# Attention and two gated layers in one kernel: state scores in column tiles, w_out converted one stage earlier

## The chip, the cores and the metric

The kernel runs on one core of a Trainium2 chip. The metric is the device time of one execution in microseconds (us), the median of several runs of the same program. Inside a core TensorE (PE in the profile) multiplies matrices, VectorE (DVE) and ScalarE (ACT) work element by element, GpSimd (POOL) does a little of the same, and the queue of SyncE (SP) issues the DMA transfers. [...]

## The reference

Eight batches, eight heads, 512 tokens x of 64 numbers and 32 state tokens per head. `xread` lets each x token read the 32 states, `sread` lets each state read the 512 x tokens. Both go through a gated layer (512 to 1536 to 512) and then through a second layer (512 to 2048 to 512):

```python
scores  = scale * x @ state.T        # first softmax, over 32 states
xread   = softmax(scores) @ state
scores2 = scale * state @ x.T        # second softmax, over 512 x tokens
sread   = softmax(scores2) @ x
x  = concat(xread, sread).reshape(4352, 512)
x  = (sigmoid(x @ w_gate) * (x @ w_val)) @ w_out
out = g(x @ w2_in) @ w2_out          # g: quadratic between -1 and 1, else 0 or h
```

The weights come in double precision. The kernel turns them into float32 itself, and most products are made of three fp32r products of high and low parts.

## The kernel before, in words

The eight batches are done in two groups of four (group 0, group 1). The program is a row of stages that share TensorE's queue:

1. **The start.** The attention of group 0. Its order is written out by hand in the table `PRE` (line 1320): each word is a step, a letter and the pair of heads. `st` transposes the state, `X` transposes x (`att_x`), `S` makes scores (`att_s`), `m` takes the maximum over 32 states and subtracts it (`att_m`), `x` is exp, `e` copies the raw scores to SBUF for the second softmax (`att_e`), `n` normalizes, `T` and `L` transpose the probabilities and split them in a high and a low part, `M` and `K` multiply the state into w_gate and w_val (`m_pair`, `m_low`), `Q` is the first quarter of the first gated step, and `p` and `j` convert a weight block.
2. **The gated pass of group 0** (`gated(0)`, line 594): 24 steps of 24 matmuls of 512 columns (line 582). Even steps end in two sigmoids on ACT (line 639), odd ones in two products on DVE (line 642) that go to HBM. In every odd step two M pairs are made (line 549) for a later step. They use the two PSUM tiles that the even step's sigmoids have just read.
3. **The output pass of group 0** (`output1(0)`, line 729): 96 slots of 6 matmuls with w_out (lines 713 to 715), whose moving side is split by ACT (`oh_hi`, line 680) and DVE (`oh_lo`, line 682). Into its slots go the attention of group 1 (`at_items`) and the second softmax of group 0 and then of group 1 (`sr_items`: `sr_e`, `sr_u`, `sr_r`, `sr_p`). `slot1` (line 1504) hands them out.
4. The gated pass and the output pass of group 1, the state tokens, and the whole second layer follow. They end at the span's end.

A weight block is converted by the class `Weights` in four moves: `load` (a DMA of 512 KB into one of `CB[0]` buffers `wraw`), `parts` (two ACT instructions, lines 158 and 159, into a buffer `ca` and one of two buffers `cy`), `join` (two DVE instructions, lines 165 and 169), and for w_out `high` (ACT, line 182) and `low` (DVE, line 188) into tiles that stay in SBUF. There are 24 blocks of w_gate and w_val, 12 of w_out, 16 of w2_out and 16 of w2_in, and they are done in the order of the list `weights.todo`.

`att_s` takes the x tokens as the stationary side, 128 at a time, and a block-diagonal matrix `bd` of states as the moving side: 16 float32 matmuls of 64 columns for a pair of heads, scores with x tokens on the partitions. `sr_e` then transposes them back (line 377), since the second softmax needs the state on the partitions.

Of the kernel before, what the change touches and what calls it, by code (L numbers as in the profile page):

```python
# [25 lines left out]
def attention_moe_moe_kernel(  # L26
# [28 lines left out]
    nc = tc.nc  # L55
# [40 lines left out]
    CB = [3, 4, 2]  # L96
    p1 = pool("p1", stack=st_p1)
    sd = p1.tile([128, 2, HP, 128], F32, tag="sd", name="sd")
    pe2 = pool("pe2", stack=st_e2)
    bd = pe2.tile([128, H, 4, 2, N], F32, tag="bd", name="bd")  # L100
# [7 lines left out]
    att_bufs, stn_tag = (4, 2, 2), "stn"  # L108
# [12 lines left out]
    ]  # L121
    w2_dram = [tc.dram_tile([128, 512], F32, name=f"w2_dram_{i}") for i in range(NM2)]
# [8 lines left out]
    class Weights:  # L131
# [91 lines left out]
    at_t = {}  # L223

    def load_state(bg):
        t = att.tile([128, H, 2, D], F32, tag=stn_tag, name="stn", bufs=att_bufs[0] if bg else 1)
        for b in range(4):
            o = slice(32 * b, 32 * b + 32)
            for r in range(2):
                nc.sync.dma_start(  # L230
                    out=t[o, :, r], in_=state[4 * bg + b].rearrange("h n d -> n h d")
                )
        return t

    def make_state(t, bg, k):


        ps = ps_tile(k).rearrange("p a f -> p (a f)")
        for h in range(H):
            nc.tensor.transpose(ps[:, 128 * h : 128 * h + 128], t[:, h], ident)  # L240

        def make_bd():
            for r in range(2):
                o = slice(64 * r, 64 * r + 64)
                bv = bd[o, :, :, r].rearrange("p h b n -> p (h b) n")
                v = ps[o].rearrange("p (c n) -> p c n", n=N)
                if r == 0:
                    nc.vector.tensor_copy(bv, v)
                else:
                    nc.scalar.activation(out=bv, in_=v, func=AF.Copy)  # L250

        def make_sd():
            for r in range(2):
                o = slice(64 * r, 64 * r + 64)
                v = ps[o].rearrange("p (k r c) -> p k r c", k=HP, r=2)[:, :, r]
                if r == 0:
                    nc.scalar.activation(out=sd[o, bg], in_=v, func=AF.Copy)
                else:
                    nc.vector.tensor_copy(sd[o, bg], v)

        return make_bd, make_sd
# [26 lines left out]
    def att_s(bg, hp, c, k):  # L288
        if c == 0:
            sc_t[bg, hp] = ps_tile(k)  # L290
        ps = sc_t[bg, hp].rearrange("p g (q e b n) -> p g q e b n", q=2, e=2, b=4)
        xT = xT_t.pop((bg, hp, c)).rearrange("p b (e q s) -> p b e q s", e=2, q=2)
        for b2 in range(2):
            for e in range(2):
                for q2 in range(2):
                    nc.tensor.matmul(
                        out=ps[:, q2, :, e ^ b2, 2 * c + b2],
                        lhsT=xT[:, b2, e, q2],
                        rhs=bd[:, 2 * hp + e, 2 * c + b2],
                        start=True,  # L300
                        stop=True,
                    )

# [4 lines left out]
    def att_m(bg, hp):  # L308
        pv = sc_t[bg, hp].rearrange("p g (c n) -> p (g c) n", n=N)
        m = att.tile([128, 32, 1], F32, tag="m", name="m", bufs=2)  # L310
        nc.vector.tensor_reduce(out=m, in_=pv, axis=AX.X, op=ALU.max)
# [4 lines left out]
        t = t_of(bg, hp).rearrange("p (q b) e n -> p q b e n", q=4)  # L316
        pv = pv.rearrange("p (q e b) n -> p q e b n", q=4, e=2)
        mv = m.to_broadcast([128, 32, N]).rearrange("p (q e b) n -> p q e b n", q=4, e=2)
        for e in range(2):
            nc.vector.tensor_tensor(  # L320
                out=t[:, :, :, e], in0=pv[:, :, e], in1=mv[:, :, e], op=ALU.subtract
            )
# [4 lines left out]

    def att_e(bg, hp):
        e2 = pe2.tile([128, 2, 512], F32, tag="e2", name="e2", bufs=4)
        nc.scalar.activation(out=e2, in_=sc_t.pop((bg, hp)), func=AF.Copy)  # L330
        e2_t[bg, hp] = e2
# [39 lines left out]
    def sr_e(bg, hp, k):  # L371
        s = e2_t[bg, hp]
        sv = s.rearrange("p g (q e c) -> p (g q) e c", q=2, e=2)
        ps = ps_tile(k)
        for e in range(2):
# [7 lines left out]
        post.append(lambda: sr_exp(s, ps, m2, r2))  # L383

    def sr_exp(s, ps, m2, r2):
        for e in range(2):
            nc.scalar.activation(
                out=s[:, e],
                in_=ps[:, e],
# [20 lines left out]
    def sr_u(bg, hp, k):  # L410
        e2 = e2_t.pop((bg, hp))
        ps = ps_tile(k)
        for e in range(2):
            for q in range(4):
                c = slice(128 * q, 128 * q + 128)
                nc.tensor.transpose(ps[:, e, c], e2[:, e, c], ident)
# [112 lines left out]
    def m_pair(k):  # L529
# [13 lines left out]
        for i in range(2):  # L543
            for b2 in range(2):
                for e in range(2):
# [5 lines left out]
                        lhsT=sd[o, bg, 2 * hq + i, 32 * b : 32 * b + 32],  # L551
# [38 lines left out]
    def gated(bg, begun=None, hooks={}):  # L590
# [4 lines left out]
        for i in range(4 * NQ):  # L595
# [19 lines left out]
            for _ in range(2):  # L615
                if i % 2 == 0 or i == 1:
                    split_ws()
                if i % 2 == 0:
                    if len(weights.first) < 2:
                        weights.parts()  # L620
                elif len(weights.mid) < weights.ahead:
                    weights.join()
# [1190 lines left out]
```

## Time and profile before

| what | value |
| --- | --- |
| median of 3 runs | 1452.36 us (1449.73 to 1454.36) |
| the profiled execution | 1457.21 us, its span 1455.4 us |
| PE busy | 1400.8 us, 96% |
| DVE busy | 896.3 us, 62% |
| ACT busy | 742.1 us, 51% |
| DMA engines busy | 60.9% |

The shares say that TensorE is the engine to watch, but they are means over stages with different limits. [...] Times below are counted from the span's start.

### The profile page before, as it was taken

What the parts mean: (1) busy time and instruction counts of PE and PEld (TensorE: products, weight loads), DVE (VectorE), ACT (ScalarE), POOL (GpSimd) and SP (SyncE); (2) the same over time, 40 slices, a digit from 0 to 9 for tenths busy, and PEclk for the clock granted to TensorE, in tenths of its full rate; (3) what the DMA queues carried; (4) which work ended last, traced back from release to release, by engine and by line L of the source; (5) the groups of instructions that cost most, each with busy time, mean ns of one, the idle gap of its engine ahead of it and who ended that gap; (6) DMA issues with size and microseconds to landing.
All of it is one profiled execution on the core that took longest, in us unless ns stands there. A gap on an engine that the chain in (4) does not pass through costs nothing. (4 is left out here: it accounts for less than half of the span.)

```text
span 1455.4 us, 23194 instructions
## 1 busy us (share of the span) xinstructions
PE 1400.8 (96%) x9008; PEld 1192.4 (82%) x9008; DVE 896.3 (62%) x1321; ACT 742.1 (51%) x1099; POOL 239.6 (16%) x140
## 2 busy tenths in 40 slices
PE   7899998899989999999999999999999999999997
PEld 7577776788757778789977888878879999999997
DVE  5555566657446653542266665656577887877775
ACT  6644555545346542322156777778864443434432
POOL 2000000000000000000007758698800000000000
PEclk9999998999999999999999999999999999999999
DMA  7355658757748985889265556966459334333342
GB/s 243 133 198 187 231 184 294 253 189 230 255 151 321 329 291 192 322 320 380 77 234 216 213 213 232 343 228 223 193 184 358 120 123 145 126 127 123 118 132 87
DMA packets 152669, 310.06 MB, mean 213 GB/s; under 512 B 16112, under 2 KB 83696, under 8 KB 151152
## 3 DMA queue, kind: packets, MB, share of 16 engines
q1 hardware_dynamic: 152296, 308.33, 60.9%
q8 instruction: 70, 1.15, 0.3%
q14 instruction: 39, 0.32, 0.1%
q10 hardware_dynamic: 264, 0.26, 0.1%
HBM read 181.01 MB, written 127.53 MB: 212 GB/s over the span
## 5 line engine op out<-in xcount | busy, mean ns | idle before, releaser
L1069 PE MATMUL u<-yc,wt 128*128 128x512 f32 x1344 | 310.4, 392 | 5.8 <-ACT m L1077 3.9
L1069 PEld LDWEIGHTS u<-yc,wt 128*128 128x128 f32 x1344 | 253.2, 189 | 62.1 <-ACT m L1077 5.5
L582 PE MATMUL ps<-at_hi,M 128*128 128x512 f32 x768 | 243.8, 393 | 0.9 <-ACT sg L639 0.9
L582 PEld LDWEIGHTS ps<-at_hi,M 128*128 128x128 f32 x768 | 144.1, 188 | 51.1 <-issue 19.3
L804 POOL TENSOR_TENSOR w2c<-w2c 128x256 f32<-128x256 f32 (+2 forms) x38 | 37.0, 987 | 723.6 <-DMA w2c<-w_dram 718.7
L713 PE MATMUL ps<-oh_hi,wo 128*128 128x512 f32 x368 | 150.3, 408 | 4.0 <-ACT oh_hi L680 4.0
L714 PE MATMUL ps<-oh_lo,wo 128*128 128x512 f32 x368 | 146.8, 399 | 5.6 <-DVE oh_lo L682 5.6
L582 PE MATMUL ps<-at_lo,M 128*128 128x512 f32 x384 | 149.9, 390 | 1.1 <-DVE at_lo L363 1.1
L715 PE MATMUL ps<-oh_hi,wo 128*128 128x512 f32 x368 | 145.9, 396 | 0.0
L1137 PE MATMUL o<-w,hc 128*128 128x256 f32 x476 | 136.0, 286 | 1.5 <-ACT w L927 1.5
L1139 PE MATMUL o<-w,hc 128*128 128x256 f32 x476 | 136.1, 286 | 1.2 <-DVE hc L1185 1.2
L1138 PE MATMUL o<-w,hc 128*128 128x256 f32 x476 | 136.2, 286 | 1.1 <-DVE w L804 1.1
L1139 PE MATMUL o<-wt,hc 128*128 128x256 f32 x476 | 134.8, 283 | 0.7 <-DVE hc L1185 0.7
L1138 PE MATMUL o<-wt,hc 128*128 128x256 f32 x476 | 134.7, 283 | 0.0
L1137 PE MATMUL o<-wt,hc 128*128 128x256 f32 x476 | 134.7, 283 | 0.0
L1181 ACT ACTIVATE hc<-hc 128x512 fp32r<-128x512 f32 (+1 forms) x108 | 64.9, 602 | 136.6 <-DMA hc<-hd_dram 124.2
L567 DVE TENSOR_TENSOR M<-ps,M 128x1024 fp32r<-128x1024 f32 x48 | 56.8, 1219 | 107.2 <-ACT M L561 107.2
L991 POOL TENSOR_TENSOR yc<-yr,yc 128x1024 fp32r<-128x1024 f32 x49 | 116.4, 2416 | 11.2 <-ACT yc L988 11.2
L1029 DVE SCALAR_TENSOR_TENSOR sg<-u,sg 128x512 f32<-128x512 f32 x96 | 66.3, 690 | 71.5 <-ACT u L1028 70.7
L1181 ACT ACTIVATE hc<-hs 128x512 fp32r<-128x512 f32 (+1 forms) x144 | 80.1, 597 | 48.7 <-DVE hs L1178 48.1
L1027 ACT ACTIVATE u<-sg,half 128x512 f32<-128x512 f32 x96 | 66.4, 692 | 71.2 <-DVE sg L1047 69.7
L682 DVE TENSOR_TENSOR oh_lo<-oh_lo,oh_hi 128x1024 fp32r<-128x1024 f32 x48 | 58.6, 1223 | 64.8 <-ACT oh_hi L680 64.8
(154 smaller groups left out, 2798.7 us busy)
## 6 DMA issues: line engine op xcount, KB each, us to landing
hd_dram<-sg SPq DMA_DIRECT2D x64, 512.0 KB, 5.0
h_dram<-sg SPq DMA_DIRECT2D x48, 512.0 KB, 4.3
oh_lo<-h_dram SPq DMA_DIRECT2D x48, 512.0 KB, 5.7
hc<-hd_dram SPq DMA_DIRECT2D x96, 256.0 KB, 4.3
yr<-y_dram SPq DMA_DIRECT2D x32, 512.0 KB, 6.8
wraw<-in_moe_w_out_dram SPq DMA_DIRECT2D x28, 512.0 KB, 5.2
ws_dram<-w SPq DMA_DIRECT2D x24, 512.0 KB, 6.0
ws<-ws_dram SPq DMA_DIRECT2D x24, 512.0 KB, 8.9
```

Source lines behind the costliest of these rows:

```text
L582: nc.tensor.matmul(out=ps[bp][:, b2], lhsT=M[:, l, b2, c], rhs=a[:, b2], start=(hq == 0 and j == 0), stop=(hq == 1 and j == 2),)
L713: nc.tensor.matmul(out=ps, lhsT=wh[:, c], rhs=hi, start=first, stop=False)
L714: nc.tensor.matmul(out=ps, lhsT=wh[:, c], rhs=lo, start=False, stop=False)
L715: nc.tensor.matmul(out=ps, lhsT=wl[:, c], rhs=hi, start=False, stop=last)
L991: low_on.tensor_tensor(out=t[:, 1, :n], in0=src, in1=f32(t[:, 0, :n]), op=SUB)
L1027: nc.scalar.activation(out=s, in_=c, func=AF.Relu, bias=half, scale=0.5)
L1029: return lambda: nc.vector.scalar_tensor_tensor(out=o, in0=s, scalar=1.0, in1=c, op0=ALU.min, op1=ALU.max)
L1069: nc.tensor.matmul(out=pm[j], lhsT=a, rhs=b, start=not more and k == 0 and i == 0, stop=k == 1 and i == 2, skip_group_check=more,)
L1137: nc.tensor.matmul(out=ps, lhsT=wh, rhs=vh, start=start and i == 0, stop=False)
L1138: nc.tensor.matmul(out=ps, lhsT=wh, rhs=vl, start=False, stop=False)
L1139: nc.tensor.matmul(out=ps, lhsT=wl, rhs=vh, start=False, stop=last)
L1181: nc.scalar.activation(out=get(j)[0], in_=raw(j), func=AF.Copy)
```

## The change

It has three parts.

**Scores by state token.** `att_s` now takes the state as the stationary side (64 rows by 32 columns, a tile of the array) and x as the moving side (256 columns): 16 matmuls on eight such tiles. Their result has the states on the partitions, so the second softmax can use it as it is: `sr_e` loses its transposes and reads SBUF. The first softmax needs the x tokens on the partitions, so a new step `A` (`att_a`) transposes the copy in SBUF that `E` (`att_e`) makes, and `m` waits for it. The block-diagonal matrix and its copies go; `sT`, the transposed state, takes their place and that of `sd`.

**State doubled on chip.** The state is loaded once (four DMAs, on ACT's queue for group 0) and copied by DVE, not loaded twice.

**w_out one stage earlier.** Blocks 4 to 11 of w_out are converted among the blocks of w_gate and w_val in `gated(0)`, put into HBM as float32 (`wof_dram`), loaded again in the first slots of the output pass (`load_wo`) and split there (`split_wo`). Blocks 0 to 3 come last in the gated pass. The blocks of w2_out follow from there. In `gated(0)` three blocks per two steps are converted, not two. The slots of the output pass that convert are now every fourth from slot 22 on, and its attention items start at slot 8, not 16. `PRE` has a new order.

```diff
-    CB = [3, 4, 2]
+    CB = [3, 5, 2]
...
         def high(self):
-            if self.mid and opened:
+            if self.mid and (opened or getattr(self.mid[0][1], "early", False)):
...
     def make_state(t, bg, k):
+        nc.vector.tensor_copy(t[:, :, 1], t[:, :, 0])
         ps = ps_tile(k).rearrange("p a f -> p (a f)")
         for h in range(H):
             nc.tensor.transpose(ps[:, 128 * h : 128 * h + 128], t[:, h], ident)
...
+        v = ps.rearrange("p (h c) -> p h c", h=H)
+        nc.vector.tensor_copy(sT[bg][:, : H // 2], v[:, : H // 2])
+        return lambda: nc.scalar.activation(
+            out=sT[bg][:, H // 2 :], in_=v[:, H // 2 :], func=AF.Copy
+        )
...
-    def att_s(bg, hp, c, k):
...
+    def att_s(bg, hp, k):
+        sc_t[bg, hp] = ps = ps_tile(k)
+        xT = [xT_t.pop((bg, hp, c)) for c in range(2)]
+        for e in range(2):
+            for b in range(4):
+                for r in range(2):
+                    o = slice(64 * r, 64 * r + 64)
+                    i = 256 * (e ^ (b % 2))
                     nc.tensor.matmul(
-                        out=ps[:, q2, :, e ^ b2, 2 * c + b2],
-                        lhsT=xT[:, b2, e, q2],
-                        rhs=bd[:, 2 * hp + e, 2 * c + b2],
+                        out=ps[32 * b : 32 * b + 32, r, i : i + 256],
+                        lhsT=sT[bg][o, 2 * hp + e, 32 * b : 32 * b + 32],
+                        rhs=xT[b // 2][o, b % 2, 256 * e : 256 * e + 256],
...
+    def att_a(bg, hp, k):
+        e2 = e2_t[bg, hp]
+        ps = ps_tile(k)
+        for e in range(2):
+            for q in range(4):
+                nc.tensor.transpose(ps[:, e, 128 * q : 128 * q + 128], e2_part(e2, e, q), ident)
+        a_t[bg, hp] = ps
...
-    def sr_e(bg, hp, k):
+    def sr_e(bg, hp):
         s = e2_t[bg, hp]
-        sv = s.rearrange("p g (q e c) -> p (g q) e c", q=2, e=2)
-        ps = ps_tile(k)
-        for e in range(2):
-            for q in range(4):
-                nc.tensor.transpose(ps[:, e, 128 * q : 128 * q + 128], sv[:, q, e], ident)
         m2 = srd.tile([128, 2], F32, tag="m2", name="m2", bufs=2)
-        nc.vector.tensor_reduce(out=m2, in_=ps, axis=AX.X, op=ALU.max)
+        nc.vector.tensor_reduce(out=m2, in_=s, axis=AX.X, op=ALU.max)
...
+            if bg == 0:
+                weights.low()
+                weights.high()
+                for _ in range(2 if i % 2 and i < 18 else 1):
+                    weights.join()
+                for _ in range(1 if i % 2 or i > 17 else 2):
+                    weights.parts()
...
+        dst.early = i < 2
+        dst.kind = "raw" if i >= 4 else "wo"
...
+    def load_wo(i):
+        nc.sync.dma_start(out=f32(wo_tiles(i)[1]), in_=wof_dram[i])
+
+    def split_wo(i):
+        hi, lo = wo_t[i]
+        nc.scalar.activation(out=hi, in_=f32(lo), func=AF.Copy)
+        nc.vector.tensor_tensor(out=lo, in0=f32(lo), in1=f32(hi), op=ALU.subtract)
...
-        "st bd X00 X01 S00 sd S01 p0 X10 X11 m0 x0 j0 e0 p1 S10 n0 S11 m1 X20 j1 X21 S20 x1 "
...
+        "st sb X00 X01 X10 S0 E0 X11 A0 p0 m0 S1 E1 X21 A1 p1 X20 X30 j0 S2 x0 m1 x1 E2 j1 n0 p2 "
...
-    weights.todo += [job_m(i) for i in range(4 * NQ)]
+    weights.todo += [job_m(i) for i in range(8)]
+    for i in range(8, 4 * NQ):
+        weights.todo += [job_wo(i // 2)] * (i % 2 == 0) + [job_m(i)]
+    weights.todo += [job_wo(i) for i in range(4)]
...
+        if n < 8:
+            load_wo(4 + n)
+        if n % 2 and 5 <= n < 20:
+            split_wo((n + 3) // 2)
...
-        if n % (2 if n < 28 or n >= 60 else 8) == 0:
+        if n >= 22 and n % 4 == 2:
             weights.slot()
```

TensorE's queue at the start, up to the second pair of heads: `stn` is the state, `xa` the x tokens, `e` the raw scores in SBUF. Before, then now:

```order
1 L240 MATMUL ps_213<-ident,stn 128x128 x8
2 L281 MATMUL ps_224<-ident,xa 128x128 x8
3 L281 MATMUL ps_238<-ident,xa 128x128 x8
4 L296 MATMUL ps_255<-bd,xT 128x2x32 x16
5 L281 MATMUL ps_278<-ident,xa 128x128 x8
6 L281 MATMUL ps_292<-ident,xa 128x128 x8
7 L296 MATMUL ps_327<-bd,xT 128x2x32 x16
```

```order
1 L238 MATMUL ps_229<-ident,stn 128x128 x8
2 L263 MATMUL ps_240<-ident,xa 128x128 x8
3 L263 MATMUL ps_254<-ident,xa 128x128 x8
4 L263 MATMUL ps_268<-ident,xa 128x128 x8
5 L280 MATMUL ps_279<-xT,sT 32x256 x16
6 L263 MATMUL ps_298<-ident,xa 128x128 x8
7 L306 MATMUL ps_309<-ident,e_296 128x128 x8
8 L280 MATMUL ps_326<-xT,sT 32x256 x16
```

The scores (L296, now L280) are followed by transposes of their copy (L306), with an x transpose of the next pair between them.

ACT's queue in two steps of the gated pass (an odd one and the even one behind it), with what each instruction waits for: `ca` and `cy` are the two instructions of `parts`, `sg` the sigmoids, `M` the copies of an M pair. Before, then now:

```order
50 L158 ACTIVATE ca<-wraw 128x512 [waits DMAHW6_49,DMAHW5_49,DMAHW4_49]
51 L159 ACTIVATE cy<-wraw 128x512 [waits DVE_49]
52 L158 ACTIVATE ca<-wraw 128x512 [waits DMAHW7_49,DMAHW1_49,DMAHW0_49]
53 L159 ACTIVATE cy<-wraw 128x512 [waits DVE_49]
54 L639 ACTIVATE sg<-ps_721 128x1024 [waits PE_49]
55 L639 ACTIVATE sg<-ps_722 128x1024 [waits PE_49]
56 L561 ACTIVATE M_786<-ps_777 128x1024 [waits PE_49]
```

```order
49 L158 ACTIVATE ca<-wraw 128x512 [waits DMAHW5_49,DMAHW1_49]
50 L159 ACTIVATE cy<-wraw 128x512 [waits DVE_49]
51 L158 ACTIVATE ca<-wraw 128x512 [waits DMAHW4_49,DMAHW3_49,DMAHW0_49]
52 L159 ACTIVATE cy<-wraw 128x512 [waits DVE_49]
53 L158 ACTIVATE ca<-wraw 128x512 [waits DMAHW6_49,DMAHW5_49,DMAHW2_49]
54 L159 ACTIVATE cy<-wraw 128x512 [waits DVE_49]
55 L642 ACTIVATE sg<-ps_774 128x1024 [waits PE_49]
56 L642 ACTIVATE sg<-ps_775 128x1024 [waits PE_49]
57 L556 ACTIVATE M_844<-ps_835 128x1024 [waits PE_49]
```

A third conversion stands ahead of the two sigmoids, and each conversion waits for a transfer and for DVE.

ACT's queue where the gated pass ends and the output pass begins: `wo` are the halves of w_out, `oh_hi` the split of the moving side, `e` the exp of the second softmax. Before, then now:

```order
130 L680 ACTIVATE oh_hi<-oh_lo_1371 128x1024
131 L182 ACTIVATE wo_0_1819<-ca 128x512
132 L182 ACTIVATE wo_1_1840<-ca 128x512
133 L182 ACTIVATE wo_2_1861<-ca 128x512
134 L158 ACTIVATE ca<-wraw 128x512
135 L159 ACTIVATE cy<-wraw 128x512
136 L680 ACTIVATE oh_hi<-oh_lo_1578 128x1024
137 L387 ACT_TABLE_LOAD
138 L387 ACTIVATE e_321,r_1839<-ps_1827,m_1836 128x512 x2
139 L182 ACTIVATE wo_3_1874<-ca 128x512
140 L158 ACTIVATE ca<-wraw 128x512
141 L159 ACTIVATE cy<-wraw 128x512
```

```order
152 L695 ACTIVATE oh_hi<-oh_lo_1483 128x1024
153 L182 ACTIVATE wo_2_1963<-ca 128x512
154 L182 ACTIVATE wo_3_1967<-ca 128x512
155 L695 ACTIVATE oh_hi<-oh_lo_1704 128x1024
156 L695 ACTIVATE oh_hi<-oh_lo_1891 128x1024
157 L678 ACTIVATE wo_4_1974<-wo_4_1975 128x512
158 L383 ACT_TABLE_LOAD
159 L383 ACTIVATE e_296,r_2040<-e_296,m_2037 128x512 x2
160 L678 ACTIVATE wo_5_1987<-wo_5_1988 128x512
```

The `ca` and `cy` instructions (L158, L159) are gone from between the splits; a single split per block of w_out (L678) is left.

## Rows read from the trace of the kernel before

**Rows 1.** Windows by stage: length, PE, PEld, DVE, ACT, POOL busy, PEclk, DMA.
```profile
0.00:57.50 57.50, 42.86 (x333) 34.61 (x333) 35.70 (x47) 37.63 (x47) 10.56 (x19) 1.00 0.60 192
57.50:201.30 143.80, 143.45 (x860) 105.36 (x861) 76.83 (x84) 67.13 (x86) 0.00 (x0) 1.00 0.57 198
201.30:401.20 199.90, 185.57 (x1417) 150.94 (x1415) 122.70 (x196) 101.54 (x148) 0.00 (x0) 0.96 0.72 238
```

**Rows 2.** Waits of PE, 201.3 to 401.2: us in total, times, longest.
```profile
PE ps L281 <- ACT ev L720: 4.2, 1, 4.2
PE ps L713 <- ACT oh_hi L680: 4.0, 2, 2.2
PE ps L714 <- DVE oh_lo L682: 3.0, 3, 1.1
```

**Rows 3.** Windows behind three waits of the output pass, columns as in Rows 1.
```profile
218.00:222.50 4.50, 3.14 (x7) 2.34 (x8) 3.71 (x6) 0.77 (x2) 0.00 (x0) 0.65 0.99 345
228.90:236.00 7.10, 6.30 (x15) 4.73 (x16) 6.73 (x9) 6.11 (x10) 0.00 (x0) 0.55 0.67 230
258.90:264.00 5.10, 5.07 (x19) 4.40 (x20) 2.58 (x8) 4.38 (x8) 0.00 (x0) 0.53 0.87 297
```

**Rows 4.** Timeline of ACT, output pass: start, length, instruction, idle before and releaser.
```profile
223.96 0.66 ACT L158 ACTIVATE ca<-wraw 128x512 f32<-128x512 f32 x1 [5.20 <-DMA wraw<-in_moe_w_out_dram]
...
256.75 0.66 ACT L158 ACTIVATE ca<-wraw 128x512 f32<-128x512 f32 x1 [1.53 <-DMA wraw<-in_moe_w_out_dram]
```

**Rows 5.** Timeline of PE, output pass: transposes of the second softmax, and scores.
```profile
252.28 1.03 PE L377 MATMUL ps<-ident,e 128*128 128x128 f32 x8
253.07 0.48 PE L713 MATMUL ps<-oh_hi,wo 128*128 128x512 f32 x1
...
282.61 3.68 PE L296 MATMUL ps<-bd,xT 128*128 128x64 f32 x32
```

**Rows 6.** Timeline of PE, gated pass: two M pairs between steps' matmuls.
```profile
96.18 0.39 PE L582 MATMUL ps<-at_hi,M 128*128 128x512 f32 x1
96.50 1.95 PE L549 MATMUL ps<-ca,sd 64*32 64x512 f32 x32
98.38 0.50 PE L582 MATMUL ps<-at_hi,M 128*128 128x512 f32 x1
```

**Rows 7.** Timeline of the start: SP's queue, PE, DVE.
```profile
0.75 3.86 SPq L230 DMA_DIRECT2D stn<-in_state_dram  x8
...
6.45 1.94 PE L240 MATMUL ps<-ident,stn 128*128 128x128 f32 x8 [6.45 <-DMA stn<-in_state_dram]
...
15.70 1.22 DVE L311 TENSOR_REDUCE m<-ps 128x32 f32<-128x1024 f32 x1 [1.46 <-PE ps L296]
...
49.49 1.23 DVE L363 TENSOR_TENSOR at_lo<-ps,at_hi 128x1024 fp32r<-128x1024 f32 x1 [0.79 <-ACT at_hi L358]
...
57.50 2.01 PE L549 MATMUL ps<-ca,sd 64*32 64x512 f32 x32 [2.57 <-ACT sg L639]
```

**Rows 8.** Timeline of the gated pass: SP's queue, ACT, DVE and PE.
```profile
102.21 0.42 SPq L148 DMA_DIRECT2D wraw<-in_moe_w_val_dram  x1
...
103.54 0.42 SPq L148 DMA_DIRECT2D wraw<-in_moe_w_val_dram  x1
...
101.80 0.69 DVE L169 SCALAR_TENSOR_TENSOR ca<-ca,cy 128x512 uint32<-128x512 uint32 x1
...
105.42 0.68 ACT L158 ACTIVATE ca<-wraw 128x512 f32<-128x512 f32 x1 [2.21 <-DMA wraw<-in_moe_w_val_dram]
...
103.74 2.35 DVE L642 TENSOR_TENSOR sg<-sg,ps 128x1024 f32<-128x1024 f32 x2
...
109.48 1.95 PE L549 MATMUL ps<-ca,sd 64*32 64x512 f32 x32
...
115.19 0.42 SPq L148 DMA_DIRECT2D wraw<-in_moe_w_val_dram  x1
...
120.70 0.66 ACT L158 ACTIVATE ca<-wraw 128x512 f32<-128x512 f32 x1 [4.50 <-DMA wraw<-in_moe_w_val_dram]
```

More of the change, by code (lines that the diff above doesn't have):

```diff
@@ L121, in attention_moe_moe_kernel @@
     ]
+    wof_dram = {i: tc.dram_tile([128, 512], F32, name=f"wof_dram_{i}") for i in range(4, NM1)}
     w2_dram = [tc.dram_tile([128, 512], F32, name=f"w2_dram_{i}") for i in range(NM2)]
@@ L228, in load_state @@
             o = slice(32 * b, 32 * b + 32)
[L229 to L232, printed above, removed]
+            eng.dma_start(out=t[o, :, 0], in_=state[4 * bg + b].rearrange("h n d -> n h d"))
         return t
     def make_state(t, bg, k):
+        nc.vector.tensor_copy(t[:, :, 1], t[:, :, 0])
         ps = ps_tile(k).rearrange("p a f -> p (a f)")
@@ L302, in att_s, with att_e, e2_part @@
                     )
+    def att_e(bg, hp):
+        e2 = pe2.tile([128, 2, 512], F32, tag="e2", name="e2", bufs=4)
+        nc.scalar.activation(
+            out=e2.rearrange("p e (r f) -> p r e f", r=2),
+            in_=sc_t.pop((bg, hp)).rearrange("p r (e f) -> p r e f", e=2),
+            func=AF.Copy,
+        )
+        e2_t[bg, hp] = e2
+    def e2_part(e2, e, q):
+        o = 256 * (q % 2) + 128 * (q // 2)
+        return e2[:, e, o : o + 128]
+    def att_a(bg, hp, k):
[5 more added lines that the diff above has]
+        a_t[bg, hp] = ps
     def t_of(bg, hp):
@@ L315, in att_m @@
             )
[L316 to L322, printed above, removed]
+        nc.vector.tensor_tensor(
+            out=t_of(bg, hp).rearrange("p c e n -> p e c n"),
+            in0=ps.rearrange("p e (c n) -> p e c n", n=N),
+            in1=m.to_broadcast([128, 32, N]).rearrange("p (e c) n -> p e c n", e=2),
+            op=ALU.subtract,
+        )
     def att_exp(bg, hp):
@@ L614, in gated @@
                             m_item(1 - v)
[L615 to L621, printed above, removed]
-                    weights.join()
+            if bg == 0:
+                weights.low()
+                weights.high()
+                for _ in range(2 if i % 2 and i < 18 else 1):
+                    weights.join()
+                for _ in range(1 if i % 2 or i > 17 else 2):
+                    weights.parts()
+            else:
+                for _ in range(2):
+                    if i % 2 == 0 or i == 1:
+                        split_ws()
+                    if i % 2 == 0:
+                        if len(weights.first) < 2:
+                            weights.parts()
+                    else:
+                        weights.join()
             weights.load()
@@ L1336, in attention_moe_moe_kernel @@
             nc.gpsimd.memset(par[32 * b : 32 * b + 32, e : e + 1], float(b % 2 == e))
+    for c in range(4, 6):
+        load_xa(0, c // 2, c % 2)
+        weights.load(c - 2)
     q_ps = []
@@ L1358, in attention_moe_moe_kernel @@
             att_exp(0, n)
-        elif c == "e":
+        elif c == "E":
             att_e(0, n)
@@ L1438, in attention_moe_moe_kernel @@
     weights.todo += [job_wi(2 * m + c) for m in (4, 5, 6, 7, 0, 1, 2, 3) for c in range(2)]
+    sgp = pool("sgp", side="right", stack=st_a)
+    evp = hp_ = pool("hp", stack=st_h)
+    gated(
+        0,
+        q_ps,
+        {
+            14: lambda: load_h(0, 0),
+            18: lambda: load_h(0, 1),
+            22: lambda: load_h(0, 2),
+            23: lambda: split_h(0, 0)(),
+        },
+    )
+    st_a.close()
+    st_wo, st_a, st_b, st_s = ExitStack(), ExitStack(), ExitStack(), ExitStack()
+    wop = pool("wop", side="right", stack=st_wo)
+    att = pool("att1", side="right", stack=st_b)
+    att_bufs, stn_tag = (2, 2, 1), "xa"
+    srd = pool("srd", stack=st_s)
     st_1 = []
@@ L1447, in state_item @@
     def state_item(k):
-        for f in make_state(st_1.pop(), 1, k):
-            f()
+        make_state(st_1.pop(), 1, k)()
         xa_next(1)
@@ L1475, in t_item @@
         return f
-    at_items = [lambda k: xa_next(0), state_item, lambda k: None]
+    at_items = [lambda k: xa_next(0), lambda k: None, state_item]
     for hp in range(HP):
@@ L1529, in attention_moe_moe_kernel @@
     opened.append(True)
-    weights.ahead = 1
-    for hp in range(2):
+    for _ in range(2):
         weights.high()
         weights.low()
-        weights.join()
-        weights.load()
-        sr_e(0, hp, 1)
-    weights.high()
-    weights.low()
-    weights.parts()
-    weights.load()
     output1(0, slot1)
```

152 lines of the change are left out of this document (54 added, 98 removed), and 4 rows, old and new, of the table PRE.

## The prediction, made before the changed kernel was run

> **What bounds the kernel now.** I read the page first: PE is busy 96% of a span of 1455.4 us, so only what shortens PE's queue or its waits can shorten the time. Then the windows by stage, cut where the change works [rows 1]. They tell three different stages apart. In the start (0 to 57.5 us) PE is busy 42.86 of 57.50 us, and DVE (35.70) and ACT (37.63) have as much reason to be the limit. In the gated pass PE is busy 143.45 of 143.80 us: nothing waits, PE alone is the bound, and DVE (76.83) and ACT (67.13) are half empty. [...]
>
> Then the waits of PE in the output pass [rows 2]: 4.0 us for the high half of the moving side, 3.0 for the low half, and one of 4.2 us for an evacuation on ACT. None of the three producers is slow. ACT and DVE take their queues in order, and ahead of what PE needs stand conversions of w_out, which wait for transfers: ACT stood 5.20 us at one and 1.53 us at another, just ahead of that evacuation [rows 4]. The windows behind such waits show the clock at 0.65, 0.55 and 0.53 [rows 3]: after each, PE runs for some microseconds at the lower level. [...]
>
> **The change part by part.** The sum is made against the profiled execution: 1457.21 us, span 1455.4, that is 1.8 us around it and 4.85 us over the median of 1452.36; differences are taken over to the median as they are.
>
> *Output pass, the conversions.* Twelve blocks leave ACT's and DVE's queues here. Eight come back as a reload of 256 KB and one split each, issued from slot 0 on, split from slot 5, used from slot 8. A matmul of 512 columns takes (12.98 - 1.95) / 48 = 0.23 us, from two gated steps with their M pairs [rows 6, 8]; a slot without items is six of them, 1.4 us, so a transfer has some 7 us before its split and PE some 4 us more; late ones would show as a wait of PE at the first slots. I let the waits for the two halves go (7.0 us) and the evacuation shrink by 3.0 of its 4.2, since the evacuation itself (1 us on ACT) stays between two batches: -10.0. The lower end is -5, if the denser items take over as ACT's backlog; the upper is -14.3, all idle time. With the waits goes the slow clock behind them: -7.2, or as little as -3 if one long wait stays.
>
> *Output pass, the scores.* 16 matmuls by 64 columns take 3.68 us for a pair of heads [rows 5]. The new ones use 64 by 32 tiles, as an M pair does: 8 matmuls of 512 columns there, 16 of 256 here, the same columns on the same eight tiles. Two M pairs take 1.95 us [rows 6], so one pair, and one set of scores, 1.0 us; if it is the number of instructions and not of columns that counts, 1.95. I take 1.1: 4 x (3.68 - 1.1) = -10.3 (-6.9 at the other end; 0 if the tiles do not run beside each other).
>
> *Output pass, the transposes.* Those of the second softmax cost 253.07 - 252.28 = 0.79 us of the queue [rows 5]. Eight sets go, four new ones (group 1's step A) come: 4 x 0.79 = -3.2. DVE's maximum of the second softmax and the exp now read SBUF in place of PSUM; they lie beside PE and cost it nothing. What is new on the path is the chain S, copy on ACT, A, maximum: each link has a slot or two, about 2 us each, but its PSUM tile is held longer, and PE's in-order queue waits when a tile is not free. I put +4 for that (0 to +9).
>
> Sum of the output pass: -10.0 - 7.2 - 10.3 - 3.2 + 4 = -26.7.
>
> *The gated pass.* Here the change adds work to two engines with room, 8 blocks of w_out and four more. The question is not their busy time but the order. Two steps take 109.48 - 96.50 = 12.98 us [rows 6, 8]. Before, the last conversion ahead of the sigmoids waited for the first of two new transfers: issued at 102.21, usable at 105.42, 3.2 us later. Now a third conversion stands there and waits for the second transfer, issued at 103.54: usable at 106.8 at the same 3.2. It also needs a `cy` buffer, which a join on DVE must free first. That join now stands behind the two products that begin at 103.74 and last 2.35 us: free at 106.1 + 2 x 0.69 = 107.5. So ACT's last conversion instruction runs from 107.5 to 108.1, and the first sigmoid ends at 109.1. The M pair that needs its PSUM tile stands at 109.48. It fits, by 0.4 us. But of ten such transfers one came 5.5 us after its issue (115.19 to 120.70) [rows 8]; with 5.5 the first sigmoid would end at 109.05 + 1.85 + 0.55 = 111.4, a wait of 1.9 us. There are nine such double steps, and the DMA traffic of each grows from 2.5 MB (two loads and two results of 512 KB, two stores of 256) to 3.25 (a load and a store more). I count two late ones: +3.8 (0 to 9 x 1.9 = +17). The last three double steps convert two blocks as before.
>
> *The start.* Four DMAs of the state leave SP's queue (3.86 us for eight) [rows 7], so the x loads start at once. PE's first transposes wait for the state until 6.45. With four issues on ACT's queue (half of 3.86) and a DVE copy (0.69, as a join's instruction of that size) I get 5.5, 1.0 earlier. One S of 3.8 becomes S, copy, A: 1.1 + 1.2 (as DVE's 1024 columns, [rows 7]) + 1.0 (eight transposes, [rows 5]) = 3.3, 0.5 less; but one more x copy now stands ahead on ACT, 1.0 more. So the first maximum on DVE starts at 15.2, not 15.70. From there to the last low half DVE does what it did, in 49.49 + 1.23 - 15.70 = 35.0 us, and one join more, 1.4: 51.6, with the gaps it had. PE needs 57.50 - 2.57 - 50.72 = 4.2 us from there to the M pair of step 1, so 55.8, and the sigmoid that it waited 2.57 us for, behind a late transfer, can be done by then: ACT's last conversion there now needs only a join, not a transfer. That is -1.7; some of DVE's gaps close, so I take -2 (-6 to +8).
>
> [...]
>
> *Behind it.* The gated pass of group 1 has 10 conversions left in place of 18, beside its PE work: 0.
>
> Sum: -26.7 + 3.8 - 2 = -24.9, so 1432.3 for an execution like the profiled one and 1452.36 - 24.9 = 1427 for the median.
>
> **The rivals.** *The gated pass becomes bound by its conversions.* Every second transfer comes late by as much as the slowest: +17 in place of +3.8, 1440. For it: ACT stood 2.21 us at the first transfer as it is, with one conversion less, and this is the pattern of all ten double steps. Against: nine of the ten came within 3.7 us.
>
> *The same, and the clock falls each time, so that the kernel is slower.* If each of nine waits is followed by a stretch as in [rows 3], 7.2 / 3 = 2.4 us, the pass loses 9 x (1.9 + 2.4) = 38.7: 1452.4 - 28.7 + 38.7 = 1462. It decides from a mean of 28.7 / 9 = 3.2 us a double step on. Against it: after the wait of 2.57 us at 57.50 the M pairs still ran at full speed (2.01 us) [rows 7], and a late sigmoid moves the next joins and loads back as well, so waits do not add up.
>
> *The start gets longer.* PE now has gaps of up to 2 us between short pieces. At the lower clock its transposes take 1.94 us in place of 1.0, as the first set does [rows 7], and links that were hidden come out: the 36 matmuls from the first quarter to the M pair at 0.23 us more, and three links by 1 us, are +11; in place of -2 that is 1440. [...]
>
> *Tiles that do not overlap.* Then the scores gain nothing: 1437. The M pair, with the same shape, speaks against it.
>
> *All waits go.* No late transfer, all 14.3 us of idle time, 5 us at the start: -14.3 - 7.2 - 10.3 - 3.2 - 5 = -40: 1412.
>
> **How the numbers follow.** My forecast has 0.60, with its own range 1414 to 1436; conversions 0.15; conversions with the clock 0.08; a longer start 0.07; tiles 0.03; all waits gone 0.07. Cutting 0.05 at the lower end and 0.1 at the upper leaves 1410 to 1444. About 0.3%, 4.4 us, is what a measurement can tell from none. Every case but one lies below 1440, and the case of the conversions reaches up to no change, so: faster 0.87, same 0.05, slower 0.08.
>
> **What would show it.** Right: in the output pass no `ca` or `cy` between the first splits, PE's waits there under 6 us, PEclk 1.00 in its first 60 us, scores at about 1.1 us, the stage some 26 us shorter; in the gated pass the wait of M pairs for sigmoids small and the stage 144 to 148 us. Wrong: waits of the M pairs in most double steps, a PEclk below 0.9 in the start, or scores near 2 us or more. If PE waits for a w_out half at slots 8 to 22, the reload was too late.

## The result, and the profile after

The changed kernel takes 1435.12 us, the median of 4 runs (1433.58 to 1436.6), beside 1453.36 for the kernel before in the same session (1449.73 to 1455.87): a ratio of 0.9876, 95% interval 0.9852 to 0.9901, 18.2 us faster. The profiled execution took 1435.38 us, its span 1433.6.

These are the windows by stage of the kernel after, cut at the same events as [rows 1]: the first pair of M pairs in the gated steps, the first slot of the output pass, the first M pair of group 1. Columns as there; PEclk is the granted clock of TensorE as a share of its full speed. It is 0.50 in before from 220 to 222, from 230 to 236 and from 260 to 263 us, within the windows of [rows 3].

```profile
0.00:59.36 59.36, 38.77 (x365) 26.91 (x365) 36.56 (x43) 37.20 (x46) 9.06 (x18) 1.00 0.58 178
59.36:211.58 152.22, 144.58 (x862) 104.71 (x861) 93.33 (x110) 82.00 (x111) 0.00 (x0) 1.00 0.73 243
211.58:383.52 171.94, 165.44 (x1389) 130.84 (x1387) 108.68 (x174) 92.56 (x133) 0.00 (x0) 1.00 0.80 262
```

The start is 1.9 us longer (59.36 - 57.50), the gated pass 8.4 (152.22 - 143.80), the output pass 28.0 shorter (171.94 - 199.90), together -17.7. The two profiled executions lie 21.8 us apart, 4.1 more. That is behind these stages, where the kernel before ran from 760 to 780 us with its clock at 0.77 and 0.89 and the one after at 1.00: about 3.4 us, an estimate from these clocks (10 x 0.23 + 10 x 0.11). That execution of before lay some 4 us above the median, so the 3.4 may be its own and not the kernel's; one execution does not show it.

The waits of PE in the output pass of the kernel after (columns as in [rows 2]):

```profile
PE ps L238 <- issue: 2.1, 1, 2.1
PE ps L306 <- ACT ev L735: 1.9, 1, 1.9
PE ps L280 <- ACT xT L267: 1.3, 1, 1.3
```

None for a half of the moving side is left, the wait behind the evacuation fell from 4.2 to 1.9 us, and the granted clock of the stage is 1.00 in place of 0.96. The longest wait left, 2.1 us at L238, is new: the transposes of group 1's state wait there for the copy of the state on DVE (L235, from 230.53 us), which stands in DVE's queue behind a split of the moving side and one of w_out. The timeline of PE in the same kernel (start, length, instruction) answers to [rows 5]:

```profile
244.58 1.09 PE L280 MATMUL ps<-xT,sT 64*32 64x256 f32 x32
245.61 0.50 PE L728 MATMUL ps<-oh_hi,wo 128*128 128x512 f32 x1
...
249.27 1.03 PE L306 MATMUL ps<-ident,e 128*128 128x128 f32 x8
250.06 0.48 PE L728 MATMUL ps<-oh_hi,wo 128*128 128x512 f32 x1
```

A pair of heads takes 245.61 - 244.58 = 1.03 us of the queue and is 1.09 long, where it was 3.68 long; a set of transposes takes 0.79 as before.

One double step of the gated pass of the kernel after, SP's queue, ACT and PE, to be held against [rows 8]:

```profile
106.77 0.42 SPq L148 DMA_DIRECT2D wraw<-in_moe_w_val_dram  x1
...
108.10 0.42 SPq L148 DMA_DIRECT2D wraw<-in_moe_w_val_dram  x1
...
109.95 0.67 ACT L158 ACTIVATE ca<-wraw 128x512 f32<-128x512 f32 x1 [2.18 <-DMA wraw<-in_moe_w_val_dram]
...
113.40 0.66 ACT L158 ACTIVATE ca<-wraw 128x512 f32<-128x512 f32 x1 [2.21 <-DMA wraw<-in_moe_w_val_dram]
...
114.51 1.92 ACT L642 ACTIVATE sg<-ps 128x1024 f32<-128x1024 f32 x2
...
115.57 2.01 PE L544 MATMUL ps<-ca,sT 64*32 64x512 f32 x32 [1.36 <-ACT sg L642]
```

The first transfer is usable 3.2 us after its issue, the second 5.3 us; the sigmoids stand behind the conversion that waits for it, and PE behind the first sigmoid. Such a wait stands in each of eight double steps, 0.70 to 1.36 us long, 7.6 in all, and a double step takes 14.1 us in the mean (13.85 to 14.51) in place of 12.98. The second transfer took 4.7 to 5.3 us in all eight. The clock stays at 1.00 here.

The start of the kernel after, ACT's queue, DVE and PE, to be held against [rows 7]:

```profile
0.75 3.60 ACTq L229 DMA_DIRECT2D stn<-in_state_dram  x4
...
9.12 0.43 DVE L235 COPY stn<-stn 128x512 f32<-128x512 f32 x1 [8.25 <-DMA xa<-in_x_dram]
...
9.65 1.94 PE L238 MATMUL ps<-ident,stn 128*128 128x128 f32 x8 [9.65 <-DMA xa<-in_x_dram]
...
19.42 1.22 DVE L316 TENSOR_REDUCE m<-ps 128x32 f32<-128x1024 f32 x1 [7.11 <-PE ps L306]
...
59.36 1.95 PE L544 MATMUL ps<-ca,sT 64*32 64x512 f32 x32
```

The state is usable at 9.1 us, PE's first transposes come 3.2 us later than before, DVE's first maximum 3.7 later. From there the start is shorter than it was, and the wait of 2.57 us at its end is gone.

### The profile page after: what moved, and what is told of

Same layout as the page of the kernel before. It is cut to its first block, busy times and chain, and to the rows that moved or that the text cites. A ratio compares the mean times of both kernels' runs of the same rounds, so it can differ in the third digit from the quotient of the medians.

```text
span 1433.6 us, 23157 instructions
## 1 busy us (share of the span) xinstructions
PE 1374.2 (96%) x9008; PEld 1161.8 (81%) x9008; DVE 896.1 (63%) x1313; ACT 741.2 (52%) x1097; POOL 238.0 (17%) x139
## 5 line engine op out<-in xcount | busy, mean ns | idle before, releaser
L728 PE MATMUL ps<-oh_hi,wo 128*128 128x512 f32 x368 | 148.2, 403 | 0.0
L730 PE MATMUL ps<-oh_hi,wo 128*128 128x512 f32 x368 | 143.7, 390 | 0.0
L695 ACT ACTIVATE oh_hi<-oh_lo 128x1024 fp32r<-128x1024 f32 x48 | 50.5, 1055 | 84.9 <-PE ps L730 42.1
```

What stands on the lines that cost most here:

```text
L728: nc.tensor.matmul(out=ps, lhsT=wh[:, c], rhs=hi, start=first, stop=False)
L730: nc.tensor.matmul(out=ps, lhsT=wl[:, c], rhs=hi, start=False, stop=last)
```

## The experiments

Each kernel was timed beside the kernel before, whose median there was 1450.3 to 1453.4 us, so the ratios are what compares them. The stages below are those of each one's profiled execution, in us; "behind" is the rest of the span, "idle" PE's idle time in the output pass (length less busy time).

```
kernel                 median   ratio to before, 95%      start  gated  output  behind  idle
before                                                    57.5   143.8  199.9   1054.2  14.3
after                  1435.1   0.9876 (0.9852 0.9901)    59.4   152.2  171.9   1050.1   6.5
e1 scores alone        1453.6   1.0008 (0.9996 1.0020)    58.9   143.3  199.1   1050.9  24.4
e2 w_out alone         1448.6   0.9975 (0.9960 0.9990)    57.2   159.6  179.9   1051.5   3.9
e3 joins first         1427.2   0.9827 (0.9808 0.9846)    60.6   143.3  173.9   1049.4   7.1
e4 state on SP         1434.2   0.9868 (0.9848 0.9888)    56.9   153.4  172.7   1043.8   7.3
e5 fourth raw          1431.7   0.9865 (0.9845 0.9886)    58.9   147.8  173.6   1049.1   6.6
e6 third cy            1437.1   0.9906 (0.9886 0.9926)    60.7   152.8  174.9   1047.8   6.4
e7 e2 + joins first    1439.6   0.9923 (0.9904 0.9942)    57.4   147.3  181.7   1053.1   5.4
e8 e3 + e4             1423.6   0.9806 (0.9785 0.9827)    59.1   143.3  172.1   1049.4   6.7
e9 e1, no transfers    1437.5   0.9895 (0.9877 0.9912)    59.8   143.3  182.5   1050.0  11.4
e10 e8, x on 2 queues  1425.5   0.9818 (0.9801 0.9834)    57.6   143.4  177.2   1052.3   7.3
```

The stages are those of one execution each. The code of the output pass is the same in e8 and e10, and it took 172.1 us in one and 177.2 in the other (1432.2 us, the slowest of e10's six), at a granted clock of 1.00 and 0.97. A difference of a few us in one stage alone shows little.

**The halves apart: e1 and e2.** e1 is the kernel after with w_out handled as before (`job_wo`, the order of `weights.todo`, the branch of `gated()` for group 0 and the lines for w_out in `slot1()` are put back), but with the fifth `ca` buffer kept. e2 is the kernel before with the new handling of w_out alone; its edit, shortened:

```
+    CB = [3, 5, 2]
...
+            if bg == 0:                                             (in gated())
+                weights.low()
+                weights.high()
+                for _ in range(2 if i % 2 and i < 18 else 1):
+                    weights.join()
+                for _ in range(1 if i % 2 or i > 17 else 2):
+                    weights.parts()
...
+        if n < 8:                                                   (in slot1())
+            load_wo(4 + n)
+        if n % 2 and 5 <= n < 20:
+            split_wo((n + 3) // 2)
```

> The changed kernel with the whole handling of w_out put back as it was (twelve blocks converted in the output pass, two conversions per double step in the first gated pass); the new scores, transposes and state stay. Theory: the two halves of the change are nearly independent, and the gain of 18.2 us over the kernel before is the sum of scores -10.3, transposes -3.2, the longer chain +4, and the start +1.9 for this half, so this kernel is 7.6 us faster than before (1445.8), with no wait of M pairs for sigmoids in the first gated pass beyond the 0.4 us of before; the waits behind w_out conversions in the output pass (ev, oh_hi, oh_lo, together 11.2 us before) and their low clock stay. Rival (the denser items make the w_out conversions worse, since they share ACT and DVE): those waits grow by 5 us or more and the kernel is within 3 us of before.

> The kernel before with only the new handling of w_out (conversion in the first gated pass, eight blocks stored and loaded again, fifth ca buffer); old scores, old state, old start. Theory: the output pass loses its waits (-10.0) and its low clock (-7.2), the first gated pass gains the waits of M pairs (+8.4 as measured in the changed kernel), the start stays within 1 us: 8.8 us faster than before, 1444.6. Rival (the low clock has another cause than the waits, such as the short score matmuls): the clock of the output pass stays at 0.96 to 0.98 and the kernel is about 2 us faster than before only, 1452.

Neither came out at its number. e1 is no faster than before, e2 is by 3.7 us, and the two together are by 18.2. For e1 the rival had the time right, within 3 us of before, but not the place: the waits at `ev`, `oh_hi` and `oh_lo` that it said would grow are 7.6 us in place of 11.2, and others come beside them. e1 takes 10.9 us out of PE's busy time in the output pass (185.57 - 174.66) and gives 10.1 back as idle time (24.4 - 14.3). Windows of the stage, the waits of PE there, and ACT's group by line (busy, mean; idle before, and what ended it), all of e1:

```profile
202.20:401.30 199.10, 174.66 (x1389) 135.11 (x1387) 132.38 (x210) 111.93 (x167) 0.00 (x0) 0.96 0.79 266
```

```profile
PE ps L306 <- ACT e L290: 6.2, 2, 3.5
PE ps L238 <- issue: 5.0, 1, 5.0
PE ps L437 <- ACT ev L715: 2.9, 1, 2.9
```

```profile
L158 ACT ACTIVATE ca<-wraw 128x512 f32<-128x512 f32 x34 | 22.6, 665 | 40.7 <-DMA wraw<-in_moe_w_in_dram 21.2 <-DMA wraw<-in_moe_w_out_dram 19.5
```

The same group in the kernel before:

```profile
L158 ACT ACTIVATE ca<-wraw 128x512 f32<-128x512 f32 x24 | 16.0, 667 | 19.9 <-DMA wraw<-in_moe_w_out_dram 19.9
```

ACT stands 40.7 us at raw transfers, where it stood 19.9, and what PE needs next, the copy of the scores above all (6.2 us in two waits), stands in order behind. One such place in e1's timeline:

```profile
251.44 0.66 ACT L158 ACTIVATE ca<-wraw 128x512 f32<-128x512 f32 x1 [1.90 <-DMA wraw<-in_moe_w_out_dram]
...
252.55 1.01 ACT L290 ACTIVATE e<-ps 128x1024 f32<-128x1024 f32 x1
...
253.62 1.09 PE L306 MATMUL ps<-ident,e 128*128 128x128 f32 x8 [2.69 <-ACT e L290]
```

Yet e1 is not the scores alone. With the fifth `ca` buffer it converts 34 blocks in this pass, and the kernel before 24; the ten more come in the last 40 us of the stage, and PE is idle 6.4 us there in place of 1.2. So about half of the 10.1 us of idle time lies beside conversions that the kernel before does later. What the new scores would be worth with four buffers, no run shows. And the wait of 5.0 us at L238 is again for the copy of the state on DVE, which stands behind a join and a split there; it belongs to the state doubled on chip and not to the scores.

In e2 the output pass gains 20.0 us, but its gated pass loses 15.8: 12.1 in nine waits for sigmoids, the rest at a low clock, 0.87 from 57 to 70 us, behind the first, and 0.89 from 170 to 185 us. So the rival of e2 fell (the output pass ran at a clock of 1.00), and the theory came near on that pass (17.2 us forecast) and was too low on the gated pass (8.4).

**Is it the transfers? e9.** This is e1 with one tile, loaded once, in place of the transfers up to slot 76, so it leaves out most weights of this pass, and its output is not that of the reference:

```
+                if fixed:
+                    self.loaded.append((fixed[0], dst))
+                    continue
```

> The kernel of e1 (new scores alone) with the weight transfers left out in the output pass up to slot 76: all conversions there read one tile that is loaded once, so their number and order on ACT and DVE stay and only their waits for transfers go (the converted weights are then not those of the reference). Theory (in e1 the 10.9 us that PE's queue lost came back as waits, because ACT stood 40.7 us at raw transfers with PE's inputs queued behind): ACT no longer stands there, PE's idle time in the output pass falls from 24.4 us to some 8, the clock is back at 1.00, and the pass is 170 to 180 us long in place of 199.1. Rival (the number of conversions is too much for ACT and DVE beside the denser items, transfers or not): idle time stays above 15 us and the pass above 188 us.

The order and nearly all the work on ACT stay (34 conversions, 28 of them from the tile); its group in the output pass now reads

```profile
L161 ACT ACTIVATE ca<-fixed 128x512 f32<-128x512 f32 x28 | 18.6, 664 | 1.5 <-DMA fixed<-in_moe_w_out_dram 1.5
```

and the stage

```profile
203.06:385.60 182.54, 171.10 (x1390) 133.24 (x1388) 131.67 (x210) 110.92 (x167) 0.00 (x0) 0.97 0.66 212
```

16.6 us shorter than in e1, with 11.4 us idle in place of 24.4: between the two expectations, on the theory's side. The transfers are most of it. Against the kernel after (171.94, with 165.44 busy) 10.6 us remain: 5.7 of busy time, at a clock of 0.97, and 4.9 of idle time, of which 1.9 are at the transposes of the state (4.0 here, 2.1 there). Whether the conversions cause the rest, this run does not show. It also takes load off the DMA engines (a share of 0.66 in place of 0.79), so it does not part ACT's waits for its own transfers from what those transfers do to others.

**What makes the gated pass wait: e3, e5, e6.** e3 changes the order in gated() for group 0:

```
+                if bg == 0 and i % 2:          (e3: ahead of the M pairs)
+                    for _ in range(2 if i < 18 else 1):
+                        weights.join()
+                    weights.load()
...
-                for _ in range(2 if i % 2 and i < 18 else 1):
+                if i % 2 == 0:
                     weights.join()
```

e5 has four raw tiles in place of three up to step 18, e6 three cy tiles in place of two.

> The changed kernel; in each odd step of the first gated pass the joins (and the loads that their raw buffers allow) stand ahead of the M pairs' low halves on DVE, in place of behind them. Theory (the three raw buffers go round too slowly: the third conversion waits for a transfer that can only be issued when a join behind the M lows has freed its buffer, and the first sigmoid stands behind that conversion): the loads are issued some 5 us earlier in each double step, the third conversion no longer waits, and the 7.6 us of M pairs' waits for sigmoids go: 6 to 8 us faster than the changed kernel, 1428. Rival (the transfers themselves are too slow, 3.25 MB in each double step on DMA engines that are busy 73% of the pass): loads are issued earlier but land as late, and the time stays within 2 us of 1435.

> The changed kernel with a fourth raw buffer for weight transfers in the first gated pass (up to step 18), the order of all work as it is. Theory (raw buffers: a load is issued only when a join has freed one of three): the third transfer of a double step is issued at the first join and not at the second, lands some 2 us earlier, and the first sigmoid starts about 2 us earlier, more than the waits of 0.7 to 1.4 us: the 7.6 us go, 1429. Rival (the second buffer of the low bits, for which a conversion waits 2.27 us in each double step, is what limits): waits as they are, 1434 to 1436.

> The changed kernel with a third buffer for the low bits (cy) in the first gated pass, three raw buffers and the order as they are. Theory (raw buffers): the wait of 2.27 us of the first conversion goes, the conversions behind it still wait for transfers whose issue hangs on the joins, and the time stays within 2 us of 1435. Rival (cy is what limits): the waits of M pairs go, 1428.

e3 does what the theory said. Its pass, and one double step on SP's queue and ACT:

```profile
60.61:203.92 143.31, 143.31 (x861) 105.65 (x861) 90.77 (x106) 82.06 (x110) 0.00 (x0) 1.00 0.75 256
```

```profile
100.00 0.42 SPq L148 DMA_DIRECT2D wraw<-in_moe_w_val_dram  x1
...
105.83 0.67 ACT L158 ACTIVATE ca<-wraw 128x512 f32<-128x512 f32 x1 [0.74 <-DMA wraw<-in_moe_w_val_dram]
...
108.42 1.03 ACT L646 ACTIVATE sg<-ps 128x1024 f32<-128x1024 f32 x1
```

PE is busy all of the 143.31 us. The second transfer still takes 5.8 us and ACT still waits 0.74 for it, but its issue moved from 108.10 to 100.00, in the same double step (from 7.0 us behind the start of the M pairs to 0.45). It is time of issue, not bandwidth, that was short (this pass moves 256 GB/s, after's 243). e3's ratio, 0.9827 (0.9808 to 0.9846), lies below that of the kernel after.

A fourth raw buffer with the order unchanged (e5) removes the waits too, but for one of 2.57 us in the first double step, which has slow matmuls behind it (2.60 us for the two M pairs, 1.95 in the next double step): the pass is 4.4 us shorter. The time, 1431.7, lies between its two expectations, and the ratio, 0.9865 (0.9845 to 0.9886), is not clear of the kernel after's, so e5 rests on the rows of this pass, where one wait is left of eight. The third cy buffer (e6) takes no wait away: PE waits 8.4 us for sigmoids (7.6 in the kernel after), and the pass is 152.78 us. The raw buffers it was: three of them go round, and their joins stood late.

**The two halves again, without that wait: e7.** This is e2 with the edit of e3.

> The kernel of e2 (the new handling of w_out alone, old scores and state) with the joins ahead of the M pairs' low halves in the first gated pass, as in e3. Theory: the 15.8 us by which e2's gated pass is longer than before (12.1 of waits for sigmoids, the rest low clock behind them) go, and the 20.0 us that its output pass gained show in full: 1432 to 1434, so that the scores, with the waits gone, are worth what is left to e3's 1427.2, 5 to 7 us, where alone (e1) they were worth nothing. Rival (the gated pass of the old form has another reason to wait, such as its four state and x buffers or the state of its queue at the start): more than 5 us of waits stay, 1440 or more.

At 1439.6 it came to the edge of the rival's figure, though not with the rival's 5 us of waits. Of the 15.8 us 12.3 went, but a wait of 2.71 us stays at its first M pairs (it was 2.57 in [rows 7]), with a slow clock behind it (0.84 from 55 to 60 us, 0.82 from 60 to 65), and the output pass gained 18.2 in place of 20.0. So the scores, with the new state and start that come with them, are worth more beside it than the 5 to 7 us I expected: from e7 to e3 the ratio falls from 0.9923 to 0.9827, some 14 us (12.4 by the medians). In the profiles the output pass gives 7.9 of them, the gated pass 4.0, and the start takes 3.2. The 3.7 us behind these stages I can't place: e7's clock is 0.98 from 386 to 600 us and e3's 1.00, but one execution of each does not show that this belongs to the kernels.

**The start: e4, e10, and both mends: e8.**

```
-    st_r = load_state(0, nc.scalar)
+    st_r = load_state(0, nc.sync)                                    (e4, e8, e10)
-        load_xa(0, c // 2, c % 2)
+        load_xa(0, c // 2, c % 2, nc.scalar if c % 2 else None)      (e10)
```

> The changed kernel with the four state transfers issued from SP ahead of the x loads, in place of from ACT beside them. Theory (the state lands late because its short rows share the DMA engines with the x loads issued at the same time): PE's first transposes start at about 6 us in place of 9.65, the first maximum on DVE at 16 to 17 in place of 19.42, and the start is 2.5 to 3.5 us shorter: 1432. Rival (x is the later input then, by the 1.9 us of four issues ahead of it, or DVE's later work takes the place): the first maximum moves by under 1.5 us, and the time stays within 1 us of 1435.

> The changed kernel with both mends: joins ahead of the low halves (e3) and the state issued from SP ahead of x (e4). Theory: the two lie in different stages and add, start about 2.5 us shorter than in e3 (57 to 58 us in place of 60.6 with its low clock, 59.4 without) and no waits of M pairs in the gated pass: 1424.5, faster than both kernels. Rival (the earlier start only moves the waits, since the first transfers of weights come later behind it): the gated pass starts with a wait and the time is that of e3, 1427.

> The kernel of e8 with the second and the fourth x tile issued from ACT's queue in place of SP's, so that x follows the state sooner. Theory (in e8 PE waited 2.5 us for x in the start, since SP issues one after the other at some 0.5 to 0.7 us each): the waits for x fall below 1 us, the first maximum on DVE moves from 14.8 to about 14, and the time is 1 us below e8's 1423.6. Rival (x is limited by the DMA engines, busy at about 1.06 of their share from 10 to 20 us, not by the issues; and what the start gains is lost to gaps of PE, after which its clock falls): within 1 us of e8.

The state's landing hangs on what is issued beside it. In e4 x comes behind it, in e10 half of x beside it; SP's queue and DVE, of e4 and then of e10:

```profile
0.75 1.88 SPq L229 DMA_DIRECT2D stn<-in_state_dram  x4
...
4.45 0.43 DVE L235 COPY stn<-stn 128x512 f32<-128x512 f32 x1 [3.58 <-DMA stn<-in_state_dram]
```

```profile
0.75 1.88 SPq L229 DMA_DIRECT2D stn<-in_state_dram  x4
...
7.45 0.43 DVE L235 COPY stn<-stn 128x512 f32<-128x512 f32 x1 [6.57 <-DMA stn<-in_state_dram]
```

The same four issues, usable at 4.45 and at 7.45 (at 9.12 in the kernel after, beside all of x): with half of x issued from ACT beside it, the state came 3.0 us later.

In e4 the first maximum on DVE starts at 15.36 in place of 19.42 and the start is 2.4 us shorter in the profile, near what was expected, though its timed median, 1434.2, is only 0.9 below the kernel after's and the intervals overlap: on the whole kernel e4 is not settled (its profiled execution, 1428.6, was the lowest of its four). e8 is settled against both kernels: 1423.6 us, 0.9806 (0.9785 to 0.9827), whose interval lies below that of the kernel after. Against e3 (0.9827) it is not: the intervals overlap, so the state's earlier issue is shown in the start's rows and not in the time of the whole kernel. e10 is 1.9 us above e8, with overlapping intervals: no gain shown, the rival's side.

## Why the prediction was right, and where it was not

The time fell, as forecast, and came to 1435 in place of 1427: inside the range, at the upper end of the forecast's own range (1414 to 1436). It fell short by 8 us because one term was too small and one had the wrong sign. By the prediction's own signs the output pass came out right and the gated pass wrong: the M pairs waited in eight of its nine double steps, and the stage took 152.2 us, not 144 to 148.

*Output pass, -26.7 forecast, -28.0 measured.* Taken in the order of e2 first and the scores behind it. The waits: PE's idle time falls from 14.3 to 3.9 us in e2, 10.4, where -10.0 was taken. The clock: busy time falls from 185.57 to 175.97 there, with the granted clock from 0.96 to 1.00, 9.6, where -7.2 was taken: what the three windows of [rows 3] lack to a clock of 1.00, 0.35 x 4.5 + 0.45 x 7.1 + 0.47 x 5.1. The whole stage lacked, by the same estimate, 0.04 x 199.90 = 8.0 us. Scores, transposes and the chain: from e2 to the kernel after 8.0 us, where -10.3 - 3.2 + 4 = -9.5 was taken. That the sum is within 1.3 us is in part luck, since the clock gave 2.4 more and the scores 1.5 less. The copy of group 1's state, which the sum put at nothing, costs the 2.1 us at L238. The reload was in time: no wait for a half of w_out.

What the sum did not say is that its terms do not stand alone. It adds the scores' -9.5 to the waits' -17.2 as if each could be had without the other. In e1 PE's 10.9 us come back as idle time, while ACT stands at transfers (about half of that beside the ten extra conversions); with the w_out part the scores, state and start are worth 14 us over the whole kernel (ratios 0.9975 and 0.9876 without and with them; e7 and e3 say the same). Two of the waits of e1's output pass, 6.2 us, are for the copy of the scores, not for the length of that copy (1.0 us) but for what stands ahead of it on ACT.

*The gated pass, +3.8 forecast, +8.4 measured.* The step that failed: "usable at 106.8 at the same 3.2". I gave the second of two transfers the latency of the first. It took 4.7 to 5.3 us, near what the slowest of ten took before. For one of 5.5 I had the first sigmoid 1.9 us late, and counted two of nine; eight came late. "Waits do not add up" failed half: each double step does wait only 0.95 in the mean, not 1.9, since the M pairs, the low halves, the joins behind them and so the next loads all move back with it, but for that reason the next wait comes again, a loop of 14.1 us. e3 and e5 cut that loop at two places. The rival of the conversions named this mechanism with 17 us; half of that came. That of the clock (1462) did not: no low clock behind these waits (1.00 in the pass, waits of 0.70 to 1.36 us). In e2, whose longest were 2.6, it did in part (0.87 from 57 to 70 us, behind the first).

*The start, -2 forecast, +1.9 measured.* The step that failed: the state at 5.5 by "four issues on ACT's queue (half of 3.86)". The issues took 3.60 us, not half, and it was usable at 9.1; from SP ahead of x, in e4, they took 1.88 and it was usable at 4.45. The rest was right: from the first maximum to the end of the last low half 35.6 us (19.42 to 55.0; I had 36.4), 4.4 to the M pair of step 1 (4.2), and no wait there.

The rival of the longer start came true in part, in other executions: the granted clock of the start is 0.94 to 0.97 in e1, e3, e4, e6, e8 and e9, and 1.00 in after, e5 and e10; with the old start (before, e2, e7) it is 1.00. (The prediction took the first set of transposes for work at the lower clock. It takes 1.94 us in place of 1.0 in before, after, e1, e3, e4, e8 and e10 alike, and the windows give a granted clock of 1.00 there, from 6.40 to 8.40 us of before and from 9.65 to 11.59 us of after.) e8 lost most in this row of its windows:

```profile
45.00:50.00 5.00, 5.00 (x27) 2.48 (x26) 2.13 (x5) 1.71 (x3) 2.26 (x2) 0.50 0.00 0
```

At this clock an M pair took 1.96 us (at 46.85) and a set of transposes 1.97 (at 48.74), where they took 1.09 each at a clock of 1.00 (at 33.24 and 38.09). By an estimate from the clock of 0.50 the 5 us of PE's work cost 2.5 more, and e8's start is 59.1 us although its state came 4.7 us earlier. In the five windows of 5 us before it (20 to 45 us) PE had been busy 2.6 to 3.9 of 5 us. In the kernel after it was busy 2.2 to 4.8 in the same windows, and the clock stayed at 1.00, so these rows do not tell when it falls.

## What to carry to other kernels

Where an engine stands at transfers ahead of work that PE needs, as ACT did in e1 (40.7 us in the output pass), time taken out of PE's queue can come back as idle time (10.1 of 10.9 us there); free that engine first, then count PE's savings. When a second and third transfer join one in a ring of buffers, take the latency of the last of them (5.3 us in the double step above, 3.2 for the first) and ask which instruction frees its buffer: moving two joins ahead of other work was worth 7 to 8 us here, with no extra memory. A small first input came later here whenever it was issued beside large ones, from either queue (usable at 7.45 and 9.12 us, and at 4.45 ahead of them). And a kernel with half of a change put back must be counted through before it is called that half alone: e1 kept one buffer, and with it ten more conversions.

## What the runs showed beyond that

Four transfers of the state, issued at the same times (0.75 to 2.63 us), were usable 3 us apart (4.45 us in e4, 7.45 in e10), by what was issued beside them. And the same instructions may run at another clock: after, e3, e5 and e6 issue the same instructions up to 50 us, and from 45 to 50 us its granted clock was 1.00 in after and e5 and 0.66 in e3 and e6.
